# Attention values of the later heads: pairs of heads in plain fp32 in two column halves, row sums from GpSimd adds, maxima from transposing reductions

## The chip, the cores and the metric

The kernel runs on one core of one Trainium2 chip. The metric is the device time of one execution in microseconds (us). Engines, as the profile names them: PE is the matrix engine (TensorE), PEld its loading of the stationary operand, DVE the vector engine, ACT the scalar engine, POOL is GpSimd, SP the queue that issues most DMAs.

## The reference

Three stages in fp32 follow each other, over 8 batches of 576 tokens with 512 features.

```
# attention, 8 heads of 64: a row sees the 64-token blocks up to its own
scores = scale * q @ k.T ; masked where block_i < block_j
attn = exp(scores - rowmax) ; attn /= (sum(attn) + 1e-9) ; x = attn @ v
# token mixing with low rank, then a two-layer network
u = x + (x.T @ U @ V).T ; x = u + relu(u @ w_ch1) @ w_ch2
# gated convolution over 5 tokens
out = (sigmoid(conv5(x)) * (x @ w_val)) @ w_out
```

## The kernel before

**Two streams on PE.** The 4608 tokens are cut into 9 groups of 512. For each group the two-layer network runs 16 steps; each step is 12 matmuls into `h` (L963) and 12 into four accumulators `acc` (L1015), all 128 rows by 512 columns in the reduced type fp32r, with each operand split into a high and a low part. Between them, at four places per step (`gap`, L1185), the attention of later batches is let in: it is a generator that is advanced at a set pace (`aim`, L1179, so many yields per gap), and a group can only start when its batch of attention is through. PE runs its instructions in the order in which the program lists them; for the other engines the framework sets the order by its own planned timeline, apart from a few marked places. After the last group comes the gated convolution (L1085 to L1132).

**Attention.** The 64 heads are taken in two ways. Heads 0 to 15 go through `slot` (L552), with queries as rows of the score tile. There the values of two heads are multiplied in plain fp32, one head into the PSUM rows 0 to 63 and the other into rows 64 to 127 (`emit_q_pv`, L526, matmuls at L542). Heads 16 to 63 go through `tick` (L845), one head a tick, and there the keys are rows and the queries columns: `emit_s_piece` (L403) makes the scores of two heads in four pieces on even ticks, five key blocks j = 0 to 4 with 576, 448, 320, 192 and 64 query columns, 1600 in all, held in two tiles of 832 and 768 columns.

**Maxima.** `emit_max_a` and `emit_max_b` (L606 to L621) take the maximum over the key blocks with four DVE operations, turn the result in 32 by 32 blocks and reduce it along the free axis to 128 rows by 18. `emit_max_c` (L623) joins the four quarters of the partitions and spreads the result; `emit_sub` (L643) subtracts it.

**Values and row sums.** From head 18 on (`FIRST_SPLIT`) the exponentials are split into `eh` and `el` (ACT cast and DVE subtraction, L687 to L690) and the values into `vhi` and `vlo` (ACT and POOL, L659 to L661). The stationary operand holds 64 value columns and 64 columns of ones, so that the lower half of the PSUM tile collects the row sums. `emit_pv` (L703) does one head in two banks, query columns 0 to 127 and 128 to 575: blocks 0, 1 and 2 of the second bank as three fp32r matmuls each, the rest in plain fp32. Each bank is copied twice by ACT, values to `xt` and sums to `lt` (L735, L736). For every second head `emit_norm_a` and `emit_norm_b` (L740, L750) turn the sums on DVE, take the reciprocal, spread it, and multiply on POOL. The heads 16 and 17 are whole in fp32.

A tick yields four times in its first loop, twice around its value banks, and in `mixing` (L887), which feeds the pair's result to the token mixing; `mix_H` (L820) writes the operands `uh` (ACT) and `ul` (POOL) of the next group.

Of the kernel before, what the change touches and what calls it, by code (L numbers as in the profile page):

```python
# [17 lines left out]
P = 128  # L18
# [4 lines left out]
def attn_moe_gate_kernel(ctx: ExitStack, tc: tile.TileContext, q, k, v, U, V, w1, w2, wval, convw, wout, out):  # L23
# [21 lines left out]
    FIRST_SPLIT = 2 * H + 2  # L45
# [137 lines left out]
    def open_late():  # L183
        stage.close()
        late["y"] = lpool("yp", 2)
        for nm in "evx":
            late[nm] = split.enter_context(tc.tile_pool(name=nm + "lp", bufs=1, side="left"))
# [35 lines left out]
    pool.tensor_tensor(fold, ident[:, 0:P // 2], ident[:, P // 2:], op=ALU.add)  # L223
    both = ac_p.tile([P, P], F32, name="both")
# [94 lines left out]
    def ones_v():  # L319
        for t in vstk:  # L320
            pool.memset(t[:, :, D:P], 1.0)

# [229 lines left out]
    def slot(u):  # L552
# [13 lines left out]
        if 0 <= u - 2 < NQ:  # L566
            with tc.high_priority():
                emit_q_pv(u - 2)
            if u % 2:
                for a in range(2):  # L570
                    load_v(u + 1 + a if u + 1 < NQ else NH)
# [33 lines left out]

    def emit_max_a(n):  # L606
# [5 lines left out]
        mxt[n] = m  # L612

    def emit_max_b(n):
        m = mxt.pop(n)
        t = rot("t")
# [31 lines left out]
    vlo = {}  # L648

    def prep_v(n):  # L650

        if not FIRST_SPLIT <= n < NH:
            return
        t = vstk[n % 2]
        vlo[n] = late["v"].tile([P, NK, D], F32R, tag="vlo", name="vlo")
        if not vhi:
            vhi[0] = late["v"].tile([P, NK, P], F32R, tag="vhi", name="vhi")
            act.copy(vhi[0][:, :, D:P], t[:, :, D:P])
        v_, h_ = t[:, :, 0:D], vhi[0][:, :, 0:D]  # L659
        hi_act(h_, v_)  # L660
        lo(pool, vlo[n], v_, h_)  # L661

    est = {}

    def emit_exp(n):
        if n < FIRST_SPLIT:
            return
        for half in range(2):
            s = stt[n][half][:, 0 if half else WHOLE:]
            act.activation(s, s, AF.Exp, scale=scale)  # L670

    def emit_est(n):

        if not NQ <= n < NH:
            return
        ss = stt.pop(n)
        for half, s in enumerate(ss):
            if n < FIRST_SPLIT:
                e = e_p.tile([P, sw[half]], F32, tag=f"e{half}", name="e")
                act.activation(e, s, AF.Exp, scale=scale)  # L680
                est[n, half] = (e,)
                continue
            skip = 0 if half else WHOLE
            if half == 0:
                ef = late["e"].tile([P, WHOLE], F32, tag="ef", name="ef")
                act.activation(ef, s[:, 0:WHOLE], AF.Exp, scale=scale)
            eh = late["e"].tile([P, sw[half] - skip], F32R, tag=f"eh{half}", name="eh")  # L687
            hi_act(eh, s[:, skip:])
            el = e_p.tile([P, sw[half]], F32R, tag=f"e{half}", name="el")[:, skip:]
            lo(vec, el, s[:, skip:], eh)  # L690
            est[n, half] = (eh, el, ef, skip)

    xts = {}
    lts = {}
# [8 lines left out]
    def emit_pv(n, c):  # L703
        b, h = divmod(n, H)
        pr, a = divmod(h, 2)
        if a == 0 and c == 0:
            xts[n // 2] = (late["x"] if n >= 3 * H and n // 2 % (NP + 2) == 0 else x_p).tile([P, S], F32, tag="xt", name="xt")
            lts[n // 2] = rot("lt", 1)
        xt, lt = xts[n // 2], lts[n // 2]
        last[0] = (own[a], xt[own[a]][0:1, 0:1])  # L710
        ps = ps_p.tile([P, 512], F32, tag="a", name="pPV")
        c0, c1 = ((0, P), (P, S))[c]
        split, whole = [], []
        for j in range(NK):
            a0 = max(c0, q0[j])
            if a0 >= c1:
                continue
            off = soff[j] - q0[j]
            rows = slice(0, P)
            o_, e_ = ps[:, a0 - c0:c1 - c0], slice(off + a0, off + c1)  # L720
            if n < FIRST_SPLIT:
                whole.append((o_, vstk[n % 2][rows, j, :], est[n, half_of[j]][0][rows, e_]))
            elif off + c1 <= WHOLE and half_of[j] == 0:
                whole.append((o_, vstk[n % 2][rows, j, :], est[n, 0][2][rows, e_]))
            else:
                eh, el, _, skip = est[n, half_of[j]]
                e_ = slice(off + a0 - skip, off + c1 - skip)
                for v_, m, t in ((vhi[0], P, eh), (vhi[0], P, el), (vlo[n], D, eh)):
                    split.append((o_[:m], v_[rows, j, 0:m], t[rows, e_]))
        todo = split + whole  # L730
# [114 lines left out]
    def tick(n, mixed, last=B * NP):  # L845
# [5 lines left out]
        if e + 1 >= NQ:  # L851
            load_v(e + 1)
# [437 lines left out]
```

## Time and profile before

| | us |
|---|---|
| time, median of 3 runs (lowest, highest) | 1433.97 (1433.51, 1435.35) |
| the profiled execution: its own time | 1437.6 |
| its span, first to last instruction | 1435.8 |
| PE busy, of the span | 1392.8 (97%) |
| DVE busy | 1026.1 (71%) |
| ACT busy | 698.5 (49%) |
| POOL busy | 317.9 (22%) |

A matmul's recorded length holds its way through the array, and the next one starts before it ends; what a matmul costs is read from one start to the next. A plain fp32 matmul is recorded as two instructions, an fp32r one as one. The page gives a mean granted clock of 0.997 for PE. The 1.8 us between time and span lie outside the first and the last instruction.

### The profile page before, as it was taken

The numbers are of one execution on the slowest core, as the hardware profiler recorded it, in microseconds if no ns is written. First come the engines' busy times: TensorE is split into PE (matmuls) and PEld (weight loads), VectorE is DVE, ScalarE is ACT, GpSimd is POOL, SyncE is SP. The second block draws the span as 40 slices with busy tenths as digits, with TensorE's granted clock in tenths as the row PEclk, the third lists the DMA queues.
The fourth block names the chain that finished last, engine by engine and source line by source line (L and its number), as shares of the span: only waits on it lengthen the run. The fifth ranks groups of instructions, "written<-read, shape, count | busy, mean of one in ns | idle before, by whom it ended". The sixth has DMA issues, their size and how long they took to land.

```text
span 1435.8 us, 20136 instructions
## 1 busy us (share of the span) xinstructions
PE 1392.8 (97%) x6762; PEld 1083.0 (75%) x6762; DVE 1026.1 (71%) x2105; ACT 698.5 (49%) x1539; POOL 317.9 (22%) x467
## 2 busy tenths in 40 slices
PE   6898978999999999999999999999999999999999
PEld 4666656777777777777777777778888888788887
DVE  5987889687777886888687787866225245499991
ACT  5775544555655555546455555555233211344342
POOL 3353441111121121112111211121032000344310
PEclk9999999999999999999999999999999999999999
DMA  6666775433343443434343333332255433223311
GB/s 110 155 156 202 226 235 140 114 84 97 90 113 84 93 106 103 98 87 125 84 99 88 110 88 99 84 97 83 87 177 170 151 104 131 75 83 101 110 52 66
DMA packets 246290, 163.58 MB, mean 114 GB/s; under 512 B 197669, under 2 KB 212261, under 8 KB 246186
## 3 DMA queue, kind: packets, MB, share of 16 engines
q1 hardware_dynamic: 243818, 161.99, 40.3%
q8 instruction: 54, 0.88, 0.3%
q10 hardware_dynamic: 2368, 0.30, 0.2%
q14 instruction: 50, 0.41, 0.1%
HBM read 134.98 MB, written 27.26 MB: 113 GB/s over the span
## 4 chain that ended last, share of the span: by engine, by line
PE 84%; DVE 6%; DMA 5%; ACT 3%; issue 1%; SPq 1%; POOL 0%; ACTq 0%; DVEq 0%; POOLq 0%
PE acc L1015 26%; PE h L963 25%; PE pPV L734 8%; PE o L1129 7%; PE val L1105 7%; PE pS L415 6%; DMA raw<-in_moe_w_ch_dram 3%; PE pG L810 1%; PE acc L1008 1%; PE pS L454 1%; DVE wa L125 1%; DVE wa L143 1%; DMA rawk<-in_k_dram 1%; PE pPV L542 1%; ACT s L469 1%
## 5 line engine op out<-in xcount | busy, mean ns | idle before, releaser
L1015 PE MATMUL acc<-hh,w 128*128 128x512 f32 x1152 | 401.5, 401 | 0.0
L1015 PEld LDWEIGHTS acc<-hh,w 128*128 128x128 f32 x1152 | 216.7, 188 | 65.4 <-issue 21.0
L963 PE MATMUL h<-uh,w1hi 128*128 128x512 f32 x576 | 237.1, 412 | 2.8 <-DVE xt L835 1.0
L963 PE MATMUL h<-uh,w1lo 128*128 128x512 f32 x576 | 226.5, 393 | 0.0
L963 PE MATMUL h<-ul,w1hi 128*128 128x512 f32 x576 | 226.0, 392 | 0.0
L1015 PE MATMUL acc<-hl,w 128*128 128x512 f32 x576 | 225.4, 391 | 0.0
L992 DVE SCALAR_TENSOR_TENSOR hl<-h,hh 128x512 fp32r<-128x512 f32 x144 | 98.5, 684 | 130.4 <-ACT hh L991 129.1
L991 ACT ACTIVATE hh<-h 128x512 fp32r<-128x512 f32 x144 | 85.8, 596 | 174.7 <-PE h L963 168.9
L963 PEld LDWEIGHTS h<-uh,w1hi 128*128 128x128 f32 x576 | 108.8, 189 | 46.6 <-issue 19.5
L97 POOL TENSOR_TENSOR vlo<-vstk,vhi 128x320 fp32r<-128x320 f32 x46 | 42.1, 916 | 457.0 <-ACT vhi L91 415.4
L963 PEld LDWEIGHTS h<-uh,w1lo 128*128 128x128 f32 x576 | 108.5, 188 | 24.2
L1015 PEld LDWEIGHTS acc<-hl,w 128*128 128x128 f32 x576 | 108.5, 188 | 19.5 <-issue 0.7
L963 PEld LDWEIGHTS h<-ul,w1hi 128*128 128x128 f32 x576 | 108.9, 189 | 18.7 <-issue 0.2
L1087 DVE SCALAR_TENSOR_TENSOR gt<-yb,cw,gt 128x516 f32<-128x516 f32 (+1 forms) x144 | 115.2, 831 | 1.4
L415 PE MATMUL pS<-tq,tk 64*128 64x320 f32 (+4 forms) x576 | 97.5, 427 | 5.0 <-ACT za L420 2.2
L97 POOL TENSOR_TENSOR yl<-yb,yh 128x512 fp32r<-128x512 f32 (+7 forms) x64 | 66.8, 1076 | 107.2 <-ACT yh L91 107.1
L420 ACT COPY s<-pS 128x320 f32<-128x320 f32 (+2 forms) x128 | 60.1, 497 | 52.3 <-PE pS L415 51.1
L97 POOL TENSOR_TENSOR ul<-xt,uh 128x512 fp32r<-128x512 f32 (+7 forms) x64 | 56.4, 888 | 93.4 <-ACT uh L91 93.2
L415 PEld LDWEIGHTS pS<-tq,tk 64*128 64x128 f32 x576 | 45.0, 185 | 41.9 <-issue 23.0
L670 ACT ACTIVATE s<-s 128x448 f32<-128x448 f32 (+1 forms) x62 | 43.8, 711 | 62.0 <-DVE s L646 61.8
L646 DVE TENSOR_TENSOR s<-s,mb 128x64 f32<-128x64 f32 (+4 forms) x160 | 67.3, 483 | 0.3
L97 DVE TENSOR_TENSOR el<-s,eh 128x448 fp32r<-128x448 f32 (+1 forms) x62 | 46.7, 787 | 17.6 <-PE pPV L734 9.8
(188 smaller groups left out, 2678.7 us busy)
## 6 DMA issues: line engine op xcount, KB each, us to landing
w<-w_s SPq DMA_DIRECT2D x144, 512.0 KB, 3.3
rawq<-in_q_dram SPq DMA_DIRECT2D x128, 72.0 KB, 2.9
out_dram<-ot SPq DMA_DIRECT2D x35, 256.0 KB, 2.0
rawk<-in_k_dram SPq DMA_DIRECT2D x124, 72.0 KB, 3.1
vstk<-in_v_dram SPq DMA_DIRECT2D x64, 128.0 KB, 2.6
raw<-in_moe_w_ch_dram SPq DMA_DIRECT2D x64, 128.0 KB, 2.8
raw<-in_moe_w_ch_dram SPq DMA_DIRECT2D x16, 512.0 KB, 3.9
w_s<-wo SPq DMA_DIRECT2D x16, 512.0 KB, 3.8
```

The costliest lines, as they stand in the source:

```text
L97: eng.tensor_tensor(o, i, f32(h), op=ALU.subtract)
L415: pe.matmul(t[:, o:o + w], tk[me, kslice(j)], tq[me, a0:a1], start=True, stop=True)
L420: act.copy(stt[n][half_of[j]][:, d:d + o], t[:, 0:o])
L646: noted(3, vec.tensor_tensor(sv(n, j), sv(n, j), mb[:, q0[j]:], op=ALU.subtract))
L734: pe.matmul(o_, l_, r_, start=(i == 0), stop=(i == len(todo) - 1))
L963: pe.matmul(ps[:, 0:n], w[:, d, fs], x[:, d, 0:n], start=(d == 0 and i == 0), stop=(d == ND - 1 and i == 2))
L991: act.activation(hh[:, 0:n], ps[:, 0:n], AF.Relu)
L992: latest[0] = vec.scalar_tensor_tensor(hl[:, 0:n], ps[:, 0:n], 0.0, f32(hh[:, 0:n]), op0=ALU.max, op1=ALU.subtract)
L1015: pe.matmul(acc[d][:, 0:n], w[:, wi, ds], x[:, 0:n], start=False, stop=(f == NF - 1 and i == 2))
L1087: vec.scalar_tensor_tensor(gt[d][:, 0:gw], y[:, d, j:j + gw], cw[:, d, j:j + 1], gt[d][:, 0:gw], op0=ALU.mult, op1=ALU.add)
L1105: pe.matmul(ps[:, 0:n], w[:, d, es], x[:, d, 0:n], start=(i == 0), stop=(i == 3 * ND - 1))
L1129: pe.matmul(ps[:m, cs], x[:, e, a:a + m], w[:, e, cs], start=(i == 0), stop=(i == 3 * ND - 1))
```

## The change

The heads 16 to 63 are multiplied with their values in pairs and in plain fp32: head 2p into PSUM rows 0 to 63, head 2p+1 into rows 64 to 127, in two banks of query columns 384 to 575 and 0 to 383. The splits of exponentials and values, the ones in the stationary operand and the copies of the sums are gone, and so is the rule for heads 16 and 17. The row sums come from four POOL additions over the key blocks, two DVE reductions with the flag `apply_transpose`, and one small matmul per head with the new matrix `quad`, into 18 spare columns of the first bank. The maxima come from two such reductions over the whole score tiles and five small operations that join the blocks. The values of a pair lie in alternating halves of the value tiles and are loaded on the even tick before. A pair's two banks are emitted on the odd tick, at its first and third yield. A tick no longer yields around its banks, and the pace is set to 52 yields a group in place of 68.

```
-    FIRST_SPLIT = 2 * H + 2
+    quad = ac_p.tile([P, D], F32, name="quad")
+    for a in range(2):
+        pool.tensor_tensor(quad[:, 32 * a:32 * a + 32], fold[:, 0:32], fold[:, 32:64], op=ALU.add)
...
-        c = D if n < NQ and n // 2 % 2 else 0
+        c = D if n // 2 % 2 else 0
...
 def emit_max_a(n):
-        m = rot("m", 1)
-        vec.tensor_tensor(m[:, P:], sv(n, 0, P), sv(n, 1), op=ALU.max)
-        for j in range(2, NK):
-            x = vec.tensor_tensor(m[:, q0[j]:], m[:, q0[j]:], sv(n, j), op=ALU.max)
+        r = tiny_p.tile([P, sum(nblk)], F32, tag="rb", name="rb")
+        for half, (o, w) in enumerate(((0, nblk[0]), (nblk[0], nblk[1]))):
+            x = vec.tensor_reduce(
+                r[:, o:o + w],
+                stt[n][half].rearrange("p (b a) -> p b a", a=BL),
+                axis=AX.X, op=ALU.max, apply_transpose=True)
 def emit_max_b(n):
-        vec.transpose(t[:, 0:P], sv(n, 0)[:, 0:P])
-        vec.transpose(t[:, P:], m[:, P:])
-        vec.reduce_max(r, t.rearrange("p (j a) -> p j a", a=32), axis=AX.X)
+        join(None, 1, 2)
+        join(None, 3, 4)
+        join(None, 1, 3)
+        join(r, 0, 1)
...
 def emit_exp(n):
+        pn, a = divmod(n, 2)
+        src = stt.pop(n)
+        if a:
+            dst = src
+        else:
+            e = late["e"] if pn % 2 and "e" in late else e_p
+            dst = [e.tile([P, w], F32, tag=f"e{h}", name="e") for h, w in enumerate(sw)]
+        for s, t in zip(src, dst):
+            act.activation(t, s, AF.Exp, scale=scale)
+def emit_sum_a(n):
+        m = rot("m", 1)[:, P:]
+        pool.tensor_tensor(m, ev(n, 0, P), ev(n, 1), op=ALU.add)
+        for j in range(2, NK):
+            pool.tensor_tensor(m[:, q0[j] - P:], m[:, q0[j] - P:], ev(n, j), op=ALU.add)
+def emit_sum_b(n):
+        for o, t in ((slice(0, P // BL), ev(n, 0)[:, 0:P]), (slice(P // BL, NB32), m)):
+            vec.tensor_reduce(r[:, o], t.rearrange("p (b a) -> p b a", a=BL), axis=AX.X, op=ALU.add, apply_transpose=True)
...
+    vbanks = ((3 * P, S), (0, 3 * P))
+    def emit_pv(pn, c):
+        if c == 0:
+            f = ps[:, c1 - c0:c1 - c0 + NB32]
+            for n, me in zip(heads, own):
+                pe.matmul(f[me], quad, sums.pop(n), start=True, stop=True)
+        for j in js:
+            a0 = max(c0, q0[j])
+            for n, me in zip(heads, own):
+                pe.matmul(ps[me, a0 - c0:c1 - c0], vpart(n)[:, j, :],
+                    est[n][half_of[j]][:, soff[j] + a0 - q0[j]:soff[j] + c1 - q0[j]],
+                    start=j == 0, stop=j == js[-1])
+        if c == 0:
+            vec.tensor_scalar(r, f, 1e-9, None, op0=ALU.add)
+            vec.reciprocal(r, r)
+            vec.transpose(rb..., r...)
+        with tc.high_priority():
+            act.copy(xt[:, c0:c1], ps[:, 0:c1 - c0])
+        if c:
+            pool.tensor_tensor(xt, xt, nrm.pop(pn), op=ALU.mult)
...
 def tick(n, mixed, last):
+        pn = n // 2 - 1
+        old = NQ <= 2 * pn < NH
+        if old and not half:
+            load_v(n - 2)
+            load_v(n - 1)
         for i in range(4):
...
+            if old and half and i % 2 == 0:
+                emit_pv(pn, i // 2)
...
+            if i == 2 and NQ <= n - 1 < NH:
+                emit_sum_b(n - 1)
...
+            emit_exp(n)
+            emit_sum_a(n)
...
-            count = 34 + 6 * EARLY
-            pace[:] = [0.0, (count if g == 0 else 8 * H + NP) / (4.0 * NF - SPARE), 0]
+            count = 34 + 4 * EARLY
+            pace[:] = [0.0, (count if g == 0 else 4 * H + 5 * NP) / (4.0 * NF - SPARE), 0]
```

## Rows read from the trace of the kernel before

**Rows 1.** The page, part 1: busy us, share of span, instructions.

```profile
PE 1392.8 (97%) x6762; PEld 1083.0 (75%) x6762; DVE 1026.1 (71%) x2105; ACT 698.5 (49%) x1539; POOL 317.9 (22%) x467
```

**Rows 2.** Stretches: busy us by engine (instructions), PE clock, DMA share, GB/s.

```profile
130.00:236.00 106.00, 88.62 (x439) 62.80 (x440) 91.72 (x164) 53.39 (x117) 39.77 (x44) 0.97 0.68 207
236.00:360.00 124.00, 122.84 (x587) 95.34 (x586) 94.40 (x219) 65.59 (x136) 17.69 (x35) 0.99 0.40 104
...
490.00:620.00 130.00, 129.85 (x636) 99.42 (x633) 101.80 (x228) 70.39 (x151) 23.73 (x44) 1.00 0.40 100
...
1000.00:1435.00 435.00, 432.02 (x1916) 354.41 (x1914) 242.41 (x378) 138.17 (x277) 87.41 (x89) 1.00 0.33 109
```

**Rows 3.** PE's waits, 250 to 1000 us: us in total, times, longest.

```profile
PE pS L415 <- ACT s L420: 1.0, 1, 1.0
PE pT L802 <- ACT lt L736: 0.5, 1, 0.5
```

**Rows 4.** PE in time (start, length): one head's values at 502 us.

```profile
502.31 0.40 PE L1015 MATMUL acc<-hh,w 128*128 128x512 f32 x1
502.54 0.38 PE L734 MATMUL pPV<-ef,vstk 128*128 128x128 f32 x2
...
505.21 0.40 PE L963 MATMUL h<-ul,w1hi 128*128 128x512 f32 x1
```

**Rows 5.** Groups by line (count, busy us, mean ns): value matmuls.

```profile
L734 PE MATMUL pPV<-eh,vhi 128*128 128x448 f32 x92 | 35.1, 382 | 0.0
```

**Rows 6.** PE in time at 131 us: two early heads, 832 columns.

```profile
131.19 0.39 PE L963 MATMUL h<-uh,w1lo 128*128 128x512 f32 x1
131.51 0.66 PE L542 MATMUL pPV<-m,vstk 128*64 128x192 f32 x8
132.00 1.15 PE L542 MATMUL pPV<-e,vstk 128*64 128x192 f32 x12
133.08 0.50 PE L963 MATMUL h<-uh,w1hi 128*128 128x512 f32 x1
133.42 0.40 PE L963 MATMUL h<-ul,w1hi 128*128 128x512 f32 x1
```

**Rows 7.** PE in time at 111 us: two early heads, 768 columns.

```profile
111.56 0.39 PE L963 MATMUL h<-uh,w1lo 128*128 128x512 f32 x1
111.88 0.65 PE L542 MATMUL pPV<-mb,vstk 128*64 128x256 f32 x4
...
113.67 0.40 PE L1008 MATMUL acc<-ul,identr 128*128 128x512 f32 x1
```

**Rows 8.** PE in time at 249 us: head 17, second bank.

```profile
249.45 2.75 PE L734 MATMUL pPV<-e,vstk 128*128 128x448 f32 x10
```

**Rows 9.** Groups by line on DVE: maxima, splits, a small copy.

```profile
L620 DVE TENSOR_REDUCE r<-t 128x18 f32<-128x576 f32 x48 | 35.9, 748 | 1.0
...
L618 DVE STREAM_TRANSPOSE t<-m 128x448 f32<-128x448 f32 x48 | 30.7, 640 | 0.6
L97 DVE TENSOR_TENSOR el<-s,eh 128x768 fp32r<-128x768 f32 x31 | 29.5, 952 | 0.2
...
L608 DVE TENSOR_TENSOR m<-s,s 128x448 f32<-128x448 f32 x32 | 19.9, 623 | 2.6 <-POOL s L597 2.6
...
L97 DVE TENSOR_TENSOR el<-s,eh 128x448 fp32r<-128x448 f32 x31 | 19.3, 622 | 17.4 <-PE pPV L734 9.8 <-ACT eh L91 7.0
...
L626 DVE COPY r<-r 64x18 f32<-64x18 f32 x48 | 10.4, 216 | 1.5
...
L617 DVE STREAM_TRANSPOSE t<-s 128x128 f32<-128x128 f32 x32 | 9.4, 293 | 23.0 <-POOL xt L754 11.6 <-POOL s L597 11.3
```

**Rows 10.** DVE's line L610, 490 to 620 us: busy us (instructions).

```profile
490.00:620.00 130.00, 11.31 (x24) 1.00 0.40 100
```

**Rows 11.** Groups by line on POOL: two-input operations of two widths.

```profile
L97 POOL TENSOR_TENSOR ul<-xt,uh 128x448 fp32r<-128x448 f32 x8 | 10.2, 1276 | 6.2 <-ACT uh L91 6.1
...
L97 POOL TENSOR_TENSOR ul<-xt,uh 128x64 fp32r<-128x64 f32 x8 | 3.3, 412 | 21.4 <-ACT uh L91 21.4
```

More of the change, by code (lines that the diff above doesn't have):

```diff
@@ L646, in emit_sub @@
             noted(3, vec.tensor_tensor(sv(n, j), sv(n, j), mb[:, q0[j]:], op=ALU.subtract))
[L648 to L661, printed above, removed]
@@ L663, in attn_moe_gate_kernel, with ev @@
     est = {}
+    def ev(n, j, a=0):
+        return est[n][half_of[j]][:, soff[j] + a:soff[j] + wid[j]]
     def emit_exp(n):
[L666 to L691, printed above, removed]
@@ L701, in hold @@
             vec.tensor_copy(f32(r)[rows][0:1, 0:GS:P, 0], x.to_broadcast([1, GS // P]))
[L703 to L710, printed above, removed]
-        ps = ps_p.tile([P, 512], F32, tag="a", name="pPV")
-        c0, c1 = ((0, P), (P, S))[c]
-        split, whole = [], []
-        for j in range(NK):
-            a0 = max(c0, q0[j])
[L716 to L730, printed above, removed]
-        if len(todo) > 1:
-            todo.append(todo.pop(1))
-        for i, (o_, l_, r_) in enumerate(todo):
-            pe.matmul(o_, l_, r_, start=(i == 0), stop=(i == len(todo) - 1))
-        act.copy(xt[own[a], c0:c1], ps[0:D, 0:c1 - c0])
-        act.copy(lt[own[a], c0:c1], ps[D:P, 0:c1 - c0])
@@ new lines, in emit_pv @@
+    def emit_pv(pn, c):
+        heads = (2 * pn, 2 * pn + 1)
+        if c == 0:
+            xts[pn] = (late["x"] if heads[0] >= 3 * H and pn % (NP + 2) == 0 else x_p).tile([P, S], F32, tag="xt", name="xt")
+        xt = xts[pn]
+        last[0] = (own[0], xt[own[0]][0:1, 0:1])
+        ps = ps_p.tile([P, 512], F32, tag="a", name="pPV")
+        c0, c1 = vbanks[c]
+        if c == 0:
+            f = ps[:, c1 - c0:c1 - c0 + NB32]
+            for n, me in zip(heads, own):
+                pe.matmul(f[me], quad, sums.pop(n), start=True, stop=True)
+        js = [j for j in range(NK) if q0[j] < c1]
+        for j in js:
+            a0 = max(c0, q0[j])
+            for n, me in zip(heads, own):
+                pe.matmul(
+                    ps[me, a0 - c0:c1 - c0],
+                    vpart(n)[:, j, :],
+                    est[n][half_of[j]][:, soff[j] + a0 - q0[j]:soff[j] + c1 - q0[j]],
+                    start=j == 0,
+                    stop=j == js[-1],
+                )
+        if c == 0:
+            r = tiny_p.tile([P, NB32], F32, tag="r0", name="r0")
+            vec.tensor_scalar(r, f, 1e-9, None, op0=ALU.add)
+            vec.reciprocal(r, r)
+            rb = nrm[pn] = rot("t")
+            vec.transpose(rb.rearrange("p (j a) -> p j a", a=32), r.rearrange("p (j o) -> p j o", o=1).to_broadcast([P, NB32, 32]))
+        with tc.high_priority():
+            act.copy(xt[:, c0:c1], ps[:, 0:c1 - c0])
+        if c:
+            for n in heads:
+                est.pop(n)
+            pool.tensor_tensor(xt, xt, nrm.pop(pn), op=ALU.mult)
@@ L848, in tick @@
         e = n - DEPTH
-        new, old = n < NH, NQ <= e < NH
-        if e + 1 >= NQ:
-            load_v(e + 1)
+        new, half = n < NH, n % 2
+        pn = n // 2 - 1
[3 more added lines that the diff above has]
+            load_v(n - 1)
         for i in range(4):
-            if new and n % 2 == 0:
+            if new and not half:
                 emit_s_piece(n // 2, i)
-            if i == (0 if n % 2 else 3) and new:
+            if old and half and i % 2 == 0:
+                emit_pv(pn, i // 2)
+            if i == (0 if half else 3) and new:
                 emit_corners(n)
                 emit_max_a(n)
+            if i == 2 and NQ <= n - 1 < NH:
+                emit_sum_b(n - 1)
             yield
@@ L869, in tick @@
             emit_sub(n, 1)
-        if old:
-            emit_pv(e, 0)
-            yield
-        if new:
             emit_exp(n)
-        if old:
-            emit_pv(e, 1)
-        prep_v(e + 1)
-        emit_est(e + 1)
-        if old:
-            if e % 2 == 1:
-                with tc.high_priority() if URG and e == H - 1 else ExitStack():
-                    emit_norm_a(e // 2)
-                    emit_norm_b(e // 2)
-            yield
+            emit_sum_a(n)
         yield from mixing(2 * e + 1, mixed, last)
```

52 lines of the change are left out of this document (26 added, 26 removed).

## The prediction

> **What bounds the kernel now.** I read the busy shares first: PE is busy for 97% of the span and the next engine, DVE, for 71% [rows 1]. Such a share is a mean, so I cut the span into stretches. In a line of that view the busy times stand in the order PE, PEld, DVE, ACT, POOL. Up to 236 us PE is not full (88.6 of 106 us) and DVE is (91.7). From 236 us on PE has 122.8 of 124, then 129.85 of 130 us, and in the last stretch 432 of 435 [rows 2]. Third, the waits of PE between 250 and 1000 us: the whole answer is two lines, 1.5 us together [rows 3]. So from about 240 us PE's own instructions set the end, and a microsecond of PE work less is a microsecond less, as long as no other engine fills up. The granted clock is 1.00 in the stretch at 490 us [rows 2]. All late value matmuls but the first lie in this full stretch.
>
> **The value matmuls before.** A timeline row gives start and recorded length; the lengths overlap, so I take starts. In plain running one matmul of the network follows the last after 0.23 us (502.31 to 502.54). One head's two banks begin at 502.54. The second matmul after them starts at 505.21, so the first of the network would stand at 505.21 - 0.23 = 504.98. One head costs 504.98 - 502.54 = 2.44 us [rows 4], a pair 4.88. There are 92 records of the `eh` by `vhi` matmul at 448 columns, two a head, so 46 heads or 23 pairs [rows 5].
>
> **After.** The first bank of a pair has 4 times 192 and once 64 query columns for each head, 832 in all; the second has 384, 256 and 128, that is 768. The early heads already do this: same fp32, same 128 by 64 stationary tiles, two heads in the two column halves, 832 columns in one bank and 768 in the other. So their rows are the price. At 131 us the network would have gone on at 131.19 + 0.23 = 131.42; it does so at 133.42 - 0.23 = 133.19: 1.77 us [rows 6]. The bank of 768 goes from 111.79 to 113.44: 1.65 us [rows 7]. Together 3.42 us. That the halves run side by side is seen against head 17, alone in the whole array: its 448, 448, 320, 192 and 64 columns, 1472, are recorded with 2.75 us [rows 8], some 1.8 ns a column, while the two early heads' 1664 columns in one bank take 1.77 us, 1.1 ns. The price also holds what the entry and exit cost: the first network matmul after the bank is recorded with 0.50 us where the next has 0.40 [rows 6].
>
> New is the small matmul with `quad`: two heads, two records each, 18 columns. Eight records (four of 192, four of 64) take 0.49 us from start to start, and twelve of 192 take 1.08, or 0.09 each; without the four long ones (0.36) the four short ones take 0.13 [rows 6]. From below, 18 of 64 columns of that is 0.04 us; from above, four records one by one at the 0.09 of a long one are 0.36. I take 0.12, close to the 0.13 of the nearest row, since so short a matmul hardly scales.
>
> A pair then costs 3.42 + 0.12 = 3.54 us against 4.88, a gain of 1.34 us, and 23 of them 30.8 us (25.3 to 32.7 with the ends of the small matmul). The pair of heads 16 and 17 was whole in fp32: its second bank is recorded with 2.75 us [rows 8], so some 2.6 us on PE; with a quarter for the 128 columns of the first bank (the same 1.8 ns each) 5.7 us for two heads, against 3.54. It lies at the edge of the stage where PE is not full, so I count 1.2 of these 2.2 us. Sum: 32.0 us of PE work less.
>
> **DVE.** Does it stay below PE? The stretch from 490 to 620 us holds the maxima of 8 heads (24 records of the three additions L610) [rows 10], so a head has 130 / 8 = 16.25 us and DVE works 101.8 / 8 = 12.7 us of them [rows 2]. Removed per head: 0.62 (L608), 11.31 / 8 = 1.41 (L610), 0.29 and 0.64 (the two turns), 0.75 (the reduction), and 0.95 + 0.62 for `el`, 5.29 us [rows 9, 10]. Added: a reduction with transposition stands nowhere in the trace. The plain one takes 748 ns for 576 columns, 1.30 ns a column, and the turn of 448 takes 640 ns, 1.43 ns [rows 9]. Taken as one pass at the reduction's price, 1600 columns of maxima cost 2.08 us and 576 of sums 0.75, together 2.83. From above, if the form does the turn and the reduction one after the other, it is 2.73 ns a column, 5.9 us for maxima and sums; from below, at the 952 ns that DVE needs for 768 columns of `el`, it is 1.24 ns a column and 2.7 us for maxima and sums [rows 9]. I take the one-pass price, that of the row of the same operation. Five small operations at 0.22 (the copy of 18 columns) add 1.08 [rows 9]. So DVE gets 3.91 - 5.29 = -1.4 us a head: 11.3 of 16.25 - 0.67 = 15.6 us, 73%. The turn of the sums at the end of a pair goes as well, and I leave that out.
>
> **POOL and ACT.** Four additions of 448, 320, 192 and 64 columns replace `vlo`. POOL's two-input operation takes 1276 ns at 448 and 412 at 64 columns [rows 11], 2.25 ns a column more; along that line the four are 1.28 + 0.99 + 0.70 + 0.41 = 3.4 us. POOL had 23.7 / 8 = 3.0 us a head [rows 2] and reaches 6.4 of 15.6 at most. The sums of a head are ready for the small matmul if POOL (3.4) and DVE (0.75) get through within the whole tick that lies between its exponentials and its pair's banks. What queues behind the additions on POOL are the fills of the masked corners of the next head, and so DVE's maxima; they have the rest of the tick. ACT (70.4 of 130 us) [rows 2] only loses: casts of `e` and `v`, copies of the sums; the exponentials keep their columns. SP's queue issues the same value loads, two a pair instead of one a head, on the even tick before their use. The pace of 52 yields a group matches the yields that eight ticks now have (8 times 4, and 5 for each of 4 pairs), as 68 did before, so groups should still end their attention shortly before they need it.
>
> **Sum.** The profiled execution took 1437.6 us, 3.6 over the median of 1433.97. 1437.6 - 32.0 = 1405.6 for a profiled execution; less the same 3.6, 1402 us. Its own range is 1396 (a little of DVE's relief before 240 us comes through, up to 4 us, and the small matmul costs 0.04) to 1410 (it costs 0.36, or a few new waits).
>
> **Rivals.** *Group starts wait for POOL.* The last `ul` of a batch is made on POOL shortly before the next group's first matmuls. If a head's additions (3.4 us) stand ahead of it at each of 6 group starts, PE waits up to 20 us: 1402 + 20 = 1422. For it: POOL runs in order, and a sum waits for its exponentials. Against: PE has no wait for POOL in the full stretch now [rows 3], and by program order the additions of the last head come half a tick earlier. 0.12.
>
> *DVE becomes the bound (slower).* The place is the tick of a head: 11.3 us with 2.83 in the new reductions. If they cost k times that, DVE passes 15.6 us at k = 2.5 and the old 16.25 at k = 2.75; at k = 3 it needs 17.0, 0.7 a head more than before, and 46 heads make 33 us: 1467. The turn followed by the reduction (k = 2.1) stays below. If POOL's additions also held DVE up for their whole 3.4 us, DVE would stand at 14.7 and k = 1.3 would be enough. Against that: DVE's two-input L608 takes 623 ns at 448 columns, no more than the one-input turn's 640 [rows 9], at POOL's 18%. 0.08.
>
> The Trainium skill speaks for the hold-up: by its page SBUF — State Buffer, section Who interferes with whom, a vector instruction with two SBUF inputs and a GpSimd instruction that reads SBUF lock each other out for the whole instruction. No row here shows such a lock; by it alone DVE would be at 14.7 us a head, still under PE, and the sum would be the same.
>
> *The halves give nothing in the new place.* The two heads' operands come from other tiles (one in place in the score tile, one in its own). If they took turns, a pair would cost about twice 3.2 us for the columns and 0.5 around them, 6.9 against 4.88; 23 pairs lose 46 us: 1480. Against it: in [rows 6, 7] the operands come from different tiles too. 0.02.
>
> *PE's gain is taken back by new waits of any kind to within noise*, 1434: 0.03. The forecast keeps 0.75.
>
> **Chances and range.** Within 0.2% (2.9 us, about what can be told from no change here): 0.03. Slower: 0.08 + 0.02 = 0.10. Faster: 0.75 + 0.12 = 0.87. The range from 1394 to 1421 holds the forecast's case and most of the group-start case, about 0.84 in all; above it lies what DVE as the bound would give.
>
> **What would show it.** Right: a pair's banks take about 1.9 (with the small matmul) and 1.65 us on PE, PE stays over 99% busy between 250 and 950 us, a head there lasts 15.6 us, and DVE falls to about 73%. Wrong: transposing reductions of 832 columns far over 1.1 us, PE waiting on DVE within ticks, `ul` late at group starts, or bank times above 2 us.

## The result, and the profile after

The changed kernel takes 1402.06 us (median of 4 runs, 1398.79 to 1404.9) where the kernel before takes 1434.66, run beside it (4 runs, 1433.51 to 1436.82). The ratio is 0.9767 [0.9752, 0.9781]. The four runs of the changed kernel have mean granted clocks of 0.995, 0.995, 0.996 and 0.998, from the longest to the shortest, so a part of the 6.1 us between them goes with the clock. The profiled execution of the changed kernel took 1404.9 us, with a span of 1403.1; that of the kernel before had a span of 1435.8, so the two traces differ by 32.7 us.

The busy line of the page, part 1, answers [rows 1].

```profile
PE 1361.5 (97%) x6912; PEld 1027.8 (73%) x6912; DVE 966.0 (69%) x2085; ACT 561.1 (40%) x1210; POOL 418.3 (30%) x613
```

PE has lost 31.3 us (1392.8 - 1361.5) and kept its share. That is the whole gain, less 1.4 us. DVE has lost 60 us and ACT 137, and neither is seen at its size in the time; whether a part of DVE's 60 us counts is a question for the experiments. Now the stretches, with the columns of [rows 2].

```profile
130.00:236.00 106.00, 94.52 (x473) 69.63 (x471) 89.79 (x170) 55.75 (x121) 42.05 (x42) 0.97 0.76 232
236.00:360.00 124.00, 119.05 (x628) 85.12 (x627) 97.02 (x231) 48.36 (x96) 42.80 (x74) 0.99 0.38 97
490.00:620.00 130.00, 129.22 (x688) 93.90 (x687) 94.45 (x236) 50.55 (x101) 40.15 (x69) 1.00 0.40 102
```

In the full stretch PE still has 129.2 of 130 us, and DVE has fallen from 101.8 to 94.45. The stretch behind 236 us is the one that changed for the worse: PE has 119 of 124 us where it had 122.8. (Ahead of it, from 130 to 236 us, PE has gained: 94.5 us against 88.6.) The waits of PE between 235 and 1000 us say where (total, times, longest).

```profile
PE pPV L721 <- DVE rb L630: 3.0, 1, 3.0
PE acc L998 <- DVE hl L975: 2.0, 1, 2.0
PE pPV L721 <- DVE x L96: 1.2, 3, 0.6
```

The two long ones, 5 us together, end at 245.4 us, at the small matmul of the first late pair, and at 259.8 us. Behind them PE hardly waits, as before [rows 3].

A pair's two banks stand in the trace in place of [rows 4]. This is PE in time, from the last network matmul ahead of the first bank (start, length).

```profile
493.71 0.39 PE L946 MATMUL h<-uh,w1lo 128*128 128x512 f32 x1
494.03 0.30 PE L721 MATMUL pPV<-rs,quad 128*64 128x18 f32 x4
494.17 0.36 PE L726 MATMUL pPV<-e,vstk 128*64 128x192 f32 x1
494.18 0.36 PE L726 MATMUL pPV<-s,vstk 128*64 128x192 f32 x1
...
495.71 0.50 PE L998 MATMUL acc<-hh,w 128*128 128x512 f32 x1
496.05 0.39 PE L998 MATMUL acc<-hl,w 128*128 128x512 f32 x1
...
498.34 0.39 PE L998 MATMUL acc<-hh,w 128*128 128x512 f32 x1
498.66 0.54 PE L726 MATMUL pPV<-e,vstk 128*64 128x384 f32 x1
...
500.44 0.39 PE L946 MATMUL h<-ul,w1hi 128*128 128x512 f32 x1
```

By the reckoning of the prediction the first bank goes from 493.71 + 0.23 to 496.05 - 0.23, 1.88 us, and the second from 498.34 + 0.23 to 500.44 - 0.23, 1.64 us. A pair costs 3.52 us against 4.88. From 280 us on every pair gives 1.87 to 1.89 and 1.63 to 1.65 us, but for three first banks of 2.12 to 2.54 us at the start of a group, which hold the short waits for `x`. The operands of the two heads, `e` and `s`, start 0.01 us apart: the column halves do run side by side.

DVE's groups of the new operations, whole span (out<-in, count, busy us, mean ns, idle before and its releaser).

```profile
L611 DVE TRANSPOSE_TENSOR_REDUCE rb<-s 128x26 f32<-128x832 f32 x32 | 32.1, 1021 | 22.1 <-ACT s L418 21.9 <-POOL za L596 0.3
L696 DVE TRANSPOSE_TENSOR_REDUCE rs<-m 128x14 f32<-128x448 f32 x48 | 30.6, 637 | 29.4 <-POOL m L689 29.4
L611 DVE TRANSPOSE_TENSOR_REDUCE rb<-s 128x24 f32<-128x768 f32 x32 | 29.4, 938 | 1.1 <-POOL s L595 1.0
...
L664 DVE TENSOR_TENSOR s<-s,mb 128x448 f32<-128x448 f32 x32 | 27.5, 860 | 0.0
...
L696 DVE TRANSPOSE_TENSOR_REDUCE rs<-e 128x4 f32<-128x128 f32 x24 | 7.2, 299 | 0.2
```

The reduction with transposition costs 1021 ns for 832 columns and 938 for 768, that is 1.22 ns a column: the price of one pass, that of the plain reduction in [rows 9] or a little less. The subtraction L664 stands here with 860 ns; the same operation took 616 before. POOL's largest addition is this:

```profile
L687 POOL TENSOR_TENSOR m<-e 128x448 f32<-128x448 f32 x24 | 28.2, 1176 | 132.3 <-ACT e L680 132.3
```

### The profile page after: what moved, and what is told of

The parts are those of the page before. It is cut to its first block, busy times and chain, and to the rows that moved or that the text cites. A ratio compares the mean times of both kernels' runs of the same rounds, so it can differ in the third digit from the quotient of the medians.

```text
span 1403.1 us, 19983 instructions
## 1 busy us (share of the span) xinstructions
PE 1361.5 (97%) x6912; PEld 1027.8 (73%) x6912; DVE 966.0 (69%) x2085; ACT 561.1 (40%) x1210; POOL 418.3 (30%) x613
## 4 chain that ended last, share of the span: by engine, by line
PE 80%; DVE 9%; DMA 5%; ACT 3%; issue 1%; SPq 1%; POOL 0%; ACTq 0%; DVEq 0%; POOLq 0%
PE acc L998 25%; PE h L946 24%; PE o L1112 7%; PE val L1088 7%; PE pS L413 6%; PE pPV L726 5%; DMA raw<-in_moe_w_ch_dram 4%; PE pS L452 1%; PE pG L801 1%; PE acc L991 1%; DVE wa L124 1%; DMA y_s<-y 1%; DVE wa L142 1%; DVE rb L611 1%; DVE s L664 1%
## 5 line engine op out<-in xcount | busy, mean ns | idle before, releaser
L96 POOL TENSOR_TENSOR ul<-xt,uh 128x512 fp32r<-128x512 f32 (+7 forms) x64 | 53.1, 835 | 134.9 <-ACT uh L90 134.8
L664 DVE TENSOR_TENSOR s<-s,mb 128x64 f32<-128x64 f32 (+4 forms) x160 | 83.1, 577 | 0.8
L611 DVE TRANSPOSE_TENSOR_REDUCE rb<-s 128x26 f32<-128x832 f32 (+1 forms) x64 | 61.5, 980 | 23.2 <-ACT s L418 21.9
L726 PE MATMUL pPV<-e,vstk 128*64 128x192 f32 (+4 forms) x384 | 74.8, 338 | 0.0
L687 POOL TENSOR_TENSOR m<-e 128x448 f32<-128x448 f32 x24 | 28.2, 1176 | 132.3 <-ACT e L680 132.3
## 6 DMA issues: line engine op xcount, KB each, us to landing
vstk<-in_v_dram SPq DMA_DIRECT2D x68, 128.0 KB, 2.6
raw<-in_moe_w_ch_dram SPq DMA_DIRECT2D x64, 128.0 KB, 2.8
```

The lines of the kernel that those rows point to most:

```text
L96: eng.tensor_tensor(o, i, f32(h), op=ALU.subtract)
L611: x = vec.tensor_reduce(r[:, o:o + w], stt[n][half].rearrange("p (b a) -> p b a", a=BL), axis=AX.X, op=ALU.max, apply_transpose=True,)
L664: noted(3, vec.tensor_tensor(sv(n, j), sv(n, j), mb[:, q0[j]:], op=ALU.subtract))
L726: pe.matmul(ps[me, a0 - c0:c1 - c0], vpart(n)[:, j, :], est[n][half_of[j]][:, soff[j] + a0 - q0[j]:soff[j] + c1 - q0[j]], start=j == 0, st ...
```

## The experiments

Each edit is against the changed kernel, but for one that is against the kernel before. Ratios are to the kernel before, run beside it on the same chip. A "group" in the text is a network group, measured from its first `identr` matmul to that of the next; the groups are numbered from the start. There is one trace of each kernel. Its early part differs by some 5 us without a difference in the time: the second group starts at 274.0 us in the change and at 269.4 in the kernel with the sums on DVE, and the medians of these two are the same (1402.06 and 1402.51).

### What the halves give: one head after the other

```diff
-        for j in js:
-            a0 = max(c0, q0[j])
-            for n, me in zip(heads, own):
+        for n, me in zip(heads, own):
+            for j in js:
+                a0 = max(c0, q0[j])
```

> Only the order within a value bank is changed: first all matmuls of one head, then all of the other, so that neighbours in PE's queue go into the same column half. Theory (the gain is that two neighbouring matmuls in different halves run at once): a pair's columns take 2 times 2.67 us in place of 2.67, so 2.7 us a pair more; 24 pairs make 64 us: about 1466, slower than the kernel before, with banks of about 3.3 and 2.9 us. Rival (the gain is the smaller number of columns and stationary loads, whatever the order; PE finds the other half's work by itself): within 5 us of 1402.

1443.52 us, ratio 1.0055 [1.004, 1.0069]. The same matmuls in another order lose 41.5 us, 1.73 for each of 24 pairs. The trace has the loss in the banks themselves; PE in time, around a first bank:

```profile
505.41 0.39 PE L946 MATMUL h<-uh,w1lo 128*128 128x512 f32 x1
505.73 0.30 PE L721 MATMUL pPV<-rs,quad 128*64 128x18 f32 x4
505.87 1.33 PE L726 MATMUL pPV<-e,vstk 128*64 128x192 f32 x7
506.88 0.38 PE L726 MATMUL pPV<-s,vstk 128*64 128x192 f32 x1
507.03 0.33 PE L726 MATMUL pPV<-e,vstk 128*64 128x192 f32 x1
...
507.25 1.25 PE L726 MATMUL pPV<-s,vstk 128*64 128x192 f32 x8
...
508.77 0.40 PE L998 MATMUL acc<-hl,w 128*128 128x512 f32 x1
```

Seven matmuls of `e` run alone for a microsecond. Then, where the queue passes from one head to the other, the two overlap for a few matmuls. The bank lasts 508.77 - 0.23 - 505.41 - 0.23 = 2.90 us instead of 1.88, the second one 2.34 instead of 1.64. So the overlap of the halves is what the gain is made of, and it needs the two heads to alternate in the queue. My theory had the right direction and 1 us a pair too much (2.7 where 1.73 were lost): it allowed no overlap at the crossing, and by the rows `s` starts at 506.88, when three records of `e` are still to come.

### The old maxima in the changed kernel

```diff
 def emit_max_a(n):
-    r = tiny_p.tile([P, sum(nblk)], F32, tag="rb", name="rb")
-    for half, (o, w) in enumerate(((0, nblk[0]), (nblk[0], nblk[1]))):
...
+    m = rot("lt", 1)
+    vec.tensor_tensor(m[:, P:], sv(n, 0, P), sv(n, 1), op=ALU.max)
+    for j in range(2, NK):
+        x = vec.tensor_tensor(m[:, q0[j]:], m[:, q0[j]:], sv(n, j), op=ALU.max)
...
 def emit_max_b(n):
...
-    join(None, 1, 2)
-    join(None, 3, 4)
-    join(None, 1, 3)
-    join(r, 0, 1)
+    vec.transpose(t[:, 0:P], sv(n, 0)[:, 0:P])
+    vec.transpose(t[:, P:], m[:, P:])
+    vec.reduce_max(r, t.rearrange("p (j a) -> p j a", a=32), axis=AX.X)
```

> The maxima of the late heads go back to the four DVE operations, the two turns and the reduction; the pairs in two halves and the POOL sums stay. Theory (PE sets the end, DVE has room): DVE gets some 0.2 to 1 us a head more, stays at 73 to 79% of the full stretch, and the time stays within 3 us of 1402. Rival (part of the gain is DVE's relief, the maxima included): DVE's time a head counts, and the time rises by 10 us or more, to 1412 and above.

1416.78 us (1416.55 to 1417.82), ratio 0.987 [0.9856, 0.9883]: 14 to 15 us of the gain are gone, though DVE is far from full. Its stretches, the one behind 236 us and the full one:

```profile
236.00:250.00 14.00, 10.75 (x47) 7.26 (x46) 12.98 (x26) 3.68 (x7) 6.71 (x12) 0.74 0.37 80
...
490.00:620.00 130.00, 128.63 (x684) 93.29 (x683) 100.34 (x229) 50.39 (x102) 40.08 (x68) 1.00 0.39 101
```

DVE stands at 100.3 of 130 us, 77%, and my theory that its work is hidden there fell. The loss is in two places. PE in time with the idle time ahead of a matmul in brackets, and what ended it:

```profile
234.96 1.86 PE L413 MATMUL pS<-tq,tk 64*128 64x448 f32 x2 [5.30 <-DVE hl L959]
...
247.54 0.23 PE L705 MATMUL pPV<-rs,quad 128*64 128x18 f32 x1 [3.25 <-DVE rs L680]
...
795.80 0.30 PE L705 MATMUL pPV<-rs,quad 128*64 128x18 f32 x4 [1.52 <-DVE x L96]
...
924.44 0.50 PE L930 MATMUL h<-uh,w1hi 128*128 128x512 f32 x1 [1.64 <-DVE xt L810]
```

The first place is the passage from the first stage, where DVE is nearly full: PE stops for 5.3 and 3.25 us. The first of these is 0.68 us in the changed kernel, and there it is ACT that PE waits for; the second is 2.98 there. But the change has a third stop, the one of 1.97 us at 259.8, which this kernel has not, so the three together are 8.55 us against 5.63. After the first stop the granted clock is 0.74 in the mean of 236 to 250 us, between the two levels of 1.2 and 2.4 GHz; in the changed kernel it is 1.00 there:

```profile
236.00:250.00 14.00, 11.02 (x62) 7.73 (x60) 12.72 (x35) 3.59 (x8) 5.25 (x10) 1.00 0.38 82
...
260.00:274.00 14.00, 14.00 (x61) 9.17 (x60) 4.43 (x11) 6.71 (x15) 5.21 (x12) 0.88 0.32 116
```

The changed kernel pays a smaller part of the same, 0.88 in a later slice behind its own two waits. That a part of the loss is the clock holds for all runs: their mean granted clocks are 0.993 to 0.994 here and 0.995 to 0.998 in the change, an estimated 4 of the 14.7 us from the means of these. The second place is the start of a group, where PE waits for DVE for 1.5 or 1.6 us (0.44 and none at the same places in the changed kernel). The lengths agree: the second group starts 1.6 us later, that group lasts 3.5 us longer, and the following four 0.8, 0.9, 2.2 and 2.5 longer, 11.5 us together, as the spans of the two traces.

What makes DVE late is not the same at the two stops of a group's start. Ahead of the one at 924.44 us DVE works from 909.5 to 924.3 without a gap, and the last `xt` comes at 923.77 behind the maxima and the subtraction of two heads; at the same place the change has gaps of 0.32 and 1.65 us. Ahead of the one at 795.80 DVE stands idle for 2.01 us: at the head of its queue a sum's reduction `rs` waits for ACT's exponentials, and `x` comes behind it. The old maxima also use two tiles, `lt` and `t`, the second shared with the turned reciprocals; no wait of DVE between 280 and 1000 us ends with the product on POOL that frees such a tile.

### The new maxima in the kernel before

The other half of the test puts `emit_max_a` and `emit_max_b` of the change into the kernel before and leaves the rest of it.

> The kernel before with the new maxima alone (two transposing reductions and five small operations). Theory (before the change PE waits 1.5 us in the full stretch, so relief of DVE is worth nothing there): within 3 us of the kernel before. Rival (the maxima are a gain of their own, of the size that they have in the changed kernel, 14 us): 1420 to 1425.

1437.52 us (11 runs, 1434.62 to 1440.53), ratio 1.0013 [1.0004, 1.0022]; the kernel before took 1436.93 beside it. So the maxima alone gain nothing. With old maxima, the pairs and the new sums gain 18.3 us (1435.12, the kernel before beside that run, less 1416.78); all together gain 32.6. The two parts don't add: some 14 us come only when both are there.

### Whose fault: GpSimd's additions or the length of the maxima

Two kernels put the additions of the sums on DVE, one with the new maxima and one with the old.

```diff
-        pool.tensor_tensor(m, ev(n, 0, P), ev(n, 1), op=ALU.add)
+        vec.tensor_tensor(m, ev(n, 0, P), ev(n, 1), op=ALU.add)
         for j in range(2, NK):
-            pool.tensor_tensor(m[:, q0[j] - P:], m[:, q0[j] - P:], ev(n, j), op=ALU.add)
+            vec.tensor_tensor(m[:, q0[j] - P:], m[:, q0[j] - P:], ev(n, j), op=ALU.add)
```

> The four additions of the row sums are made by DVE in place of POOL. Theory (PE sets the end; POOL's additions hold up DVE's subtraction L664, 860 ns at 448 columns in place of 616): DVE gets about 1.9 us a head of additions and the subtraction falls back to about 616 ns; DVE goes to 80 to 84% of the full stretch, PE stays full, and the time stays within 4 us of 1402. Rival (DVE is already close to setting the end): 1.5 us a head or more, 1402 + 46 x 0.5 = 1425 and above. Rival on the hold-up (the subtraction is slower for another reason, as its place in time): L664 stays near 860 ns.

With the new maxima: 1402.51 us, ratio 0.9774 [0.9761, 0.9788], the same as the change. Its full stretch:

```profile
490.00:620.00 130.00, 129.84 (x702) 94.81 (x699) 103.30 (x270) 51.93 (x104) 16.28 (x36) 1.00 0.40 101
```

DVE has 103.3 us, 79%, more than in the kernel with old maxima that lost 14 us, and nothing is lost. In this kernel the 448-column subtraction is back near its old price:

```profile
L664 DVE TENSOR_TENSOR s<-s,mb 128x448 f32<-128x448 f32 x32 | 20.9, 654 | 0.0
```

It is 654 ns without POOL's additions and 860 with them, so these do hold this two-input operation up; but the equal times show that the hold-up is worth nothing here. The Trainium skill states such a lock on its page SBUF — State Buffer, section Who interferes with whom; these two means agree that POOL's additions hold the subtraction up; whether for the whole of an instruction they do not say.

> The old maxima, as in the run that took 1417, and the four additions of the sums on DVE, as in the run that took 1402. DVE then has more work than in either, some 84% of the full stretch. Theory (the 14 us of the old maxima come from POOL's additions, which hold up the four two-input operations of the old maxima): without additions on POOL the 14 us go, 1401 to 1407, although DVE has more to do. Rival (the old maxima cost by their own length, ahead of urgent work in DVE's queue): 1415 or more, with the added work 1420.

With the old maxima: 1419.71 us, ratio 0.9877 [0.9864, 0.9891]. The loss stays when POOL's additions go, so these additions are not its cause; it goes with the old maxima.

### More of the new maxima

The last test of DVE runs the reductions with transposition several times over, with the same result: twice, as here, and with a 4 in place of the 2.

```diff
-        for half, (o, w) in enumerate(((0, nblk[0]), (nblk[0], nblk[1]))):
+        for half, (o, w) in list(enumerate(((0, nblk[0]), (nblk[0], nblk[1])))) * 2:
```

> The two maximum reductions of each head are made twice. DVE gets 1.96 us a head more, 13.8 of 16.0 us. Theory (PE sets the end while DVE's time a head is below PE's): within 4 us of 1402. Rival (what counts is when DVE comes to an urgent piece, such as the operands of a group start, and each further DVE work lengthens that, as the old maxima did with 14 us at a lower share of 77%): 1410 to 1425, with PE waits on DVE at the group starts.

1410.99 us, ratio 0.9827 [0.98, 0.9854]: 2 us more work a head cost 9 us in all, 0.19 for each of 48 heads, and the theory allowed 4. DVE has 109.97 of 130 us in the full stretch, 85%. The one long wait of it stands at the first late pair (line waited for: total, times, longest):

```profile
PE pPV L721 <- DVE rs L696: 6.4, 2, 5.8
```

By the means of the lines the doubled maxima take 4.8 us of DVE a head, the old ones 3.5 and the new ones 2.9. The longest lose 9 us and the old ones 14.7, so the length of the maxima alone does not set the loss.

> The two transposing maximum reductions of each head are made four times over, with the same result. Each costs 1.02 + 0.94 = 1.96 us, so DVE gets 5.9 us a head more: 11.8 + 5.9 = 17.7 us where a head now has 16.0. Theory (DVE becomes the bound where its own time a head passes PE's): 1.7 us a head more or a little above, 46 heads make 78 us: 1470 to 1500, PE at 85 to 92% in the full stretch. Rival (room is lost earlier, by waits within a tick): far above, 1520 or more; or (reductions overlap with other work): 1402 to 1420.

1505.84 us, ratio 1.0487 [1.0469, 1.0504]. The full stretch shows what a bound by DVE looks like:

```profile
490.00:620.00 130.00, 121.67 (x601) 86.31 (x602) 123.01 (x243) 47.54 (x95) 39.30 (x67) 0.97 0.35 89
```

DVE has 95%, PE 94%, and there are 601 matmuls in the stretch instead of 688. The kernel is 104 us longer, 2.2 us a head for 5.9 us of added work (3 x 1.96). So beyond its room DVE's work costs what passes it and more (2.2 us a head, where 1.7 pass by the expectation). Below it the loss does not follow the amount: 0 at 79% with the sums on DVE, 14.7 us at 77% with the old maxima, 9 at 85% here. What is left is where the work stands in DVE's queue; no run changes that order alone.

### Fewer changes of the tiling

The first network matmul behind a bank is recorded with 0.50 us and the next with 0.39, so going in and out of the halves costs something. One kernel puts both banks of a pair in one burst, one puts the score pieces two by two, one does both. In one more, both banks in one burst go with the sums on DVE.

```diff
-            if new and not half:
+            if new and not half and i % 2 == 0:
                 emit_s_piece(n // 2, i)
+                emit_s_piece(n // 2, i + 1)
-            if old and half and i % 2 == 0:
-                emit_pv(pn, i // 2)
+            if old and half and i == 0:
+                emit_pv(pn, 0)
+                emit_pv(pn, 1)
```

The upper half of this is the second kernel, the lower half the first.

> A pair's two value banks follow each other directly, at one yield in place of two, so PE changes between whole-array and two-half work once a pair and not twice. The two bursts cost 1.88 + 1.64 = 3.52 us where 1600 columns in four passes need 2.67 at 2.4 GHz and the small matmul 0.1, so a burst costs some 0.37 us around its columns. Theory (entry and exit are paid once per burst): 0.37 us less a pair, 24 pairs make 9 us: about 1393. Rival (the cost lies between matmuls, or PE waits for the second PSUM tile): within 3 us of 1402 or slower.

1400.87 us (1398.85 to 1403.32), ratio 0.9753 [0.9733, 0.9772]; not told apart from the change. PE in time, around a burst:

```profile
492.27 0.39 PE L947 MATMUL h<-uh,w1lo 128*128 128x512 f32 x1
492.58 0.30 PE L721 MATMUL pPV<-rs,quad 128*64 128x18 f32 x4
...
495.90 0.39 PE L999 MATMUL acc<-hl,w 128*128 128x512 f32 x1
```

It lasts from 492.50 to 495.67, 3.17 us against 3.52: 0.35 of the expected 0.37 us is saved in each pair, 8.4 in all. Some 5 of them are seen in the profiled executions (spans 1397.9 and 1403.1), and 1 in the medians. The fourth to the sixth group are shorter by 1.4, 0.7 and 1.0 us (126.4, 127.3 and 126.7 against 127.8, 128.0 and 127.7), the seventh by 2.5 (105.7 against 108.2). A part of this is only where the limit of a group falls: in the change the second bank of a pair stands behind each group's start, here the whole pair stands ahead of it. So the seventh group has one bank of 1.64 us less to do, and the second one more, which takes up what its pairs save.

The second group, which starts 4.7 us earlier, takes 136.8 us against 131.4 and ends no earlier than in the change. The trace has the reason. DVE in time, then PE and the clock:

```profile
320.95 0.65 DVE L696 TRANSPOSE_TENSOR_REDUCE rs<-m 128x14 f32<-128x448 f32 x1 [1.91 <-POOL m L689]
321.52 0.65 DVE L976 SCALAR_TENSOR_TENSOR hl<-h,hh 128x512 fp32r<-128x512 f32 x1
```

```profile
322.23 0.80 PE L413 MATMUL pS<-tq,tk 64*128 64x320 f32 x2 [1.14 <-DVE hl L976]
```

```profile
322.00:328.00 6.00, 5.78 (x16) 3.03 (x17) 2.36 (x6) 1.35 (x3) 0.00 (x0) 0.72 0.28 89
```

At the head of DVE's queue the reduction of a sum waits 1.91 us for POOL's additions; `hl`, which stands behind it, comes late, though its operand `hh` from ACT is there at 318.8, and by the profile PE stops for it. Behind the stop the granted clock falls, in the slice from 324 to 326 us to 0.50, which is the level of 1.2 GHz. The same follows a stop of 0.79 us at 387.30, with a mean clock of 0.57 from 388 to 392 us. In the change both slices have 1.00, and its second group has one stop, of 0.23 us. From 269 to 406 us PE stands still for 2.0 us, where the change has 0.2, and the two slices of low clock are an estimated 3.4 us of work: together some 5 of the 5.4 us. The Trainium skill says on its page TensorEngine Tiling (Array Packing), section Key Properties, that changing the tiling mode drains the engine; the 0.35 us for one in-and-out less agrees.

> The four score pieces of a pair are emitted two at a time, with all four PSUM tiles of the attention at once. They use the array in two row halves and are left with the same 0.50 us first matmul, so two bursts fewer a pair. Theory (0.37 us a burst): 0.74 us a pair, 24 pairs make 18 us: about 1384. Rival (with all four PSUM tiles taken, PE waits for ACT's copies, four of 0.5 us, or other attention work waits for a tile): 1400 or slower, with new waits of PE on ACT.

1413.75 us, ratio 0.9845 [0.9829, 0.9861]: 12 us slower than the change. PE in time, around such a burst, and then two single bursts in the changed kernel:

```profile
515.33 0.39 PE L947 MATMUL h<-uh,w1lo 128*128 128x512 f32 x1
515.65 2.44 PE L413 MATMUL pS<-tq,tk 64*128 64x448 f32 x8
...
518.36 0.40 PE L999 MATMUL acc<-hl,w 128*128 128x512 f32 x1
```

```profile
511.18 0.40 PE L946 MATMUL h<-uh,w1lo 128*128 128x512 f32 x1
511.51 1.02 PE L413 MATMUL pS<-tq,tk 64*128 64x448 f32 x4
...
512.79 0.40 PE L998 MATMUL acc<-hl,w 128*128 128x512 f32 x1
...
513.71 0.39 PE L998 MATMUL acc<-hh,w 128*128 128x512 f32 x1
514.03 0.81 PE L413 MATMUL pS<-tq,tk 64*128 64x320 f32 x4
...
515.11 0.39 PE L998 MATMUL acc<-hl,w 128*128 128x512 f32 x1
```

One burst of two pieces costs 2.57 us, the two alone 1.15 + 0.94 = 2.09. The entry is saved and more is lost inside the burst, within the records of its matmuls. The pair's other burst is cheaper than its two pieces (1.91 to 2.11 us against 1.38 + 0.93 = 2.31), but a pair's two bursts make 4.48 to 4.68 us between 417 and 520 us, where the four of the change make 4.40. That the matmuls wait inside a burst for score tiles which ACT has not yet copied out is likely and was not tried.

The larger part of the loss is a stop of PE in one burst of each group:

```profile
449.64 0.65 DVE L696 TRANSPOSE_TENSOR_REDUCE rs<-m 128x14 f32<-128x448 f32 x1 [1.89 <-POOL m L689]
```

```profile
450.91 0.80 PE L413 MATMUL pS<-tq,tk 64*128 64x320 f32 x2 [1.56 <-DVE hl L976]
```

It is the chain of the second group above: POOL's additions, a waiting reduction at the head of DVE's queue, `hl` behind it, PE. It comes again at 582.0, 711.8 and 841.4 us, with stops of 1.31, 1.56 and 1.56 us and the same wait of 1.89 us on DVE. These four groups last 2.5, 1.8, 1.6 and 2.0 us longer than in the change.

> Both of these: value banks of a pair in one burst, score pieces two at a time. Theory: the gains add, 9 + 18 = 27 us: about 1375. Rival: the waits of the two add, and it is no faster than the better one alone.

1414.2 us, ratio 0.9846 [0.9829, 0.9862]: the loss of the score bursts, without the gain of the banks. The stops are the same four, of 1.58, 1.59, 1.57 and 1.46 us, but here the granted clock falls to its lower level behind each of them, with the score bursts alone only behind the first. The mean clocks of the runs say the same, 0.987 to 0.989 against 0.990 to 0.994; from the difference of their means, 0.004, I estimate 6 us, most of the 8.4 that the banks save.

> The changed kernel with a pair's two banks in one burst and the sums' additions on DVE. The burst saves 0.35 us a pair (3.52 to 3.17), 8.4 us in all; in the run with the burst alone 5 us of that were lost again in the first group after 270 us. Theory (that loss comes from DVE being late at the first pairs): DVE has more work there now, so the loss stays and the time is 1397 to 1402. Rival (the loss comes from DVE's operations being held up by POOL): it goes, 1393 to 1395.

1397.07 us (1394.48 to 1399.49), ratio 0.972 [0.9706, 0.9733]. It is the fastest kernel of this study, and its interval lies below that of the change. Its second group takes 132.1 us, not 136.8, although DVE does more: where the kernel with POOL's sums stops for 1.14 and 0.79 us, it stops for 0.18 and 0.23, and the mean granted clock is 1.00 from 271 to 404 us. With the additions on DVE the reduction no longer waits for POOL. So the time lies in the range of my theory (1397 to 1402), but its cause is wrong: the loss goes with POOL's sums, by a wait on them, and the rival, which had POOL as the cause, put it down to the hold-up of operations. By the medians the burst saves 5.4 of 8.4 us here (1402.51 - 1397.07); where the other 3 go is open.

## Why the prediction was right

**PE sets the end.** Right. PE lost 31.3 us of busy time, and the span 32.7. The sum was 32.0. By groups it is 2.4 us ahead of the second group (1.2 were predicted for the pair of heads 16 and 17 and up to 4 for DVE's relief), then 5.9, 4.8, 5.7, 4.9, 5.4 and 3.7, and nothing in the last: four pairs of 1.36 us make 5.4. The first of these numbers is inside what the early part differs by from trace to trace, so the 1.2 us are not shown by themselves.

**The price of a pair from the early heads' rows.** Right: 1.88 and 1.64 us where [rows 6, 7] gave 1.77 + 0.12 and 1.65. The small matmul adds 1.88 - 1.77 = 0.11. The experiment with one head after the other shows that the overlap of the halves carries the gain, and that the early rows could be taken over because both kernels alternate the heads.

**A head lasts 15.6 us.** The gain a head was right (133.1 - 127.8 = 5.3 us in a group of 8 heads, 0.66 a head), the length was not: 127.8 / 8 = 16.0 us. I had divided a window of 130 us by the 8 heads whose maxima fell into it; the group starts give 16.6 for the kernel before.

**DVE.** Its share was 94.45 of 130, 73% as predicted. The reductions took 1.96 us for the maxima and 0.94 for the sums of a head, where I had 2.08 and 0.75. The relief is 16.6 x 101.8 / 130 less 16.0 x 94.45 / 130, 1.4 us a head, the predicted value.

**That DVE's part is worth nothing but a little ahead of 240 us.** This step failed as a reason, though its size in the sum did no harm. I had taken PE's 32 us for the work of the pairs alone, with DVE merely staying under its bound. With old maxima DVE stays under it too (77%), and 14.7 us are missing. The room of 23% is a mean: what PE waits for at a group's start and at the first late pair stands in DVE's queue behind other work, and with the old maxima it comes later. The amount is not the reason: the additions of the sums on DVE cost nothing at 79%, and the doubled new maxima, longer than the old ones, cost less than these. Whether it is the order of the queue or the form of the old operations stays open. That the change brought the new maxima along with the pairs, and so met a condition which the sum did not have, is luck: with the old ones the same sum of 32 would have stood against 18.3 us. Why the kernel before carried the same maxima without waits [rows 3] is not shown; its PE needs 0.66 us more a head, and the chain of the new sums (POOL, then DVE, then the small matmul) is not in it.

**POOL.** 40.15 of 130 us, 31%; the four additions take 1.18 + 0.88 + 0.61 + 0.32 = 3.0 us, predicted 3.4. The rival of group starts that wait for POOL did not come: in the changed kernel PE has no wait for POOL between 235 and 1000 us. The hold-up of DVE came (860 against 654 ns), at no price. What the prediction did not think of is that a sum's reduction waits for POOL at the head of DVE's queue, 28.2 us in 25 times between 280 and 1000 us; in the change PE does not stop behind it from 260 us on, in the kernels with longer bursts and POOL's sums it does.

**The rivals.** DVE as the bound has the shape that I gave it, since with the reductions four times over DVE is full; the single price k was 0.94 (1.22 against 1.30 ns a column), so it was far away. That the halves give nothing is excluded by 1.88 us. New waits did come, 5 us at 245 and 260 us, and took back far less than the gain.

## What to carry to other kernels

Where another part of the same program already runs the form that a change brings in, its rows price the change better than any reckoning, if the order of the queue is the same: two column halves overlap only where their matmuls alternate. An engine with 25% of free time can still hold up the one that sets the end, so ask of each operation what it waits for and what stands behind it in its queue at the few places where the other engine's next work is just in time. And test two parts of a change together and apart, since here 18.3 and -0.6 us make 32.6.

## What the runs showed that I had not expected

- A reduction with transposition costs 1.22 ns a column (1021 ns for 832, 938 for 768), no more than the plain one's 1.30, so in these rows the turn comes free with it.
- A two-input subtraction on DVE lengthens from 654 to 860 ns, 31%, beside POOL's additions of 3.0 us a head; the maximum L646 with 18 columns goes from 235 to 332 ns. Both are means with the additions on DVE and on POOL.
- In and out of the column halves costs 0.35 us around a bank; but of a pair's two score bursts of double length one is 0.48 us slower than two short ones, and what the other saves is less.
- After a stop of PE of 5.3 us the mean granted clock is 0.74 over 14 us, where without that stop it is 1.00; behind the change's own stops of 2.98 and 1.97 us it is 0.88 at 260 to 274 us. A wait ahead of PE can cost more than its own length: a stop of 1.14 us at 322 us, with both banks in one burst, is followed by a mean clock of 0.72 over 6 us.
- A reduction that waits for another engine holds up what stands behind it in DVE's queue: 1.89 us of waiting for POOL became stops of PE of 1.31 to 1.56 us, once a group.
